# Retention, ELU MLP and maxout MLP on one core: weight conversion in four VectorE operations, tables moved ahead of the sums' loads, masks ahead of the updates

## The chip, the core and the metric

The kernel runs on one core of one Trainium2 chip. The metric is the device time of one execution in microseconds (us); the kernel before was timed in three runs, whose median counts.

## The reference, cut to what matters

```python
def _attn_ref(q, k, v):                          # B, H, S, D = 4, 8, 768, 64
    for t in range(S):
        state = gamma[None, :, None, None] * state + np.einsum('bhd,bhe->bhde', k[:, :, t], v[:, :, t])
        y[:, :, t] = scale * np.einsum('bhd,bhde->bhe', q[:, :, t], state)

def _moe_ref(x, w_in, w_out):                    # 512 -> 2048 -> 512
    h = x @ w_in
    g = np.where(h > 0.0, h, np.exp(np.minimum(h, 0.0)) - 1.0)
    return g @ w_out

def _moe2_ref(x, w1, w2, w3, w_out):             # 512 -> 768 (three times) -> 512
    return np.maximum(np.maximum(x @ w1, x @ w2), x @ w3) @ w_out

x = _attn_ref(q, k, v).transpose(0, 2, 1, 3).reshape(3072, 512)
out = _moe2_ref(_moe_ref(x, w_in, w_out), w1, w2, w3, w_out2)
```

q, k and v are float32; the weights come as 64-bit floats, so a weight is two 32-bit words in memory.

## The kernel before, in words

**Attention.** The 3072 tokens are 24 chunks of 128 (four sequences of six). A chunk is loaded by `load` (lines 90 and 98, on the SP queue). `keys_of` (L249, GpSimd) makes the decayed keys kd, `queries_of` (L260) the decayed queries qd. On TensorE a chunk takes `quarter_scores` (L271), `quarter_update` (L301, keys times values for the state), `quarter_values` (L341) and `past` (L328, queries times the earlier state). On VectorE `quarter_mask` (L283) multiplies the scores by the decay mask into the tile a, which `quarter_values` reads, and `carry` (L311 to L318) brings the state forward. `finish` (L356 on ScalarE, L359 on VectorE) writes the result as a high and a low part, xh and xl. Scores, updates, values and the MLP's hidden product hp take their PSUM from the same four-bank pool.

**MLP.** Matmuls run in fp32r. Every operand stands as a high and a low part, and a product is three passes: high by high, high by low, low by high. For a block b of 512 tokens and a group f of 128 hidden units, `h1` makes hp with 12 matmuls (L446), then e = exp on ScalarE (L453), a Relu (L454), the ELU on VectorE (L455), its high part gh on ScalarE (L456) and its low part gl on VectorE (L459). `o1` adds gh and gl times w_out into four accumulators with 12 matmuls (L478). At the end of a run of groups, `x2_out` adds the accumulators to earlier sums (L495) and, where a block is complete, stores them to the DRAM buffer x2d (L501, SP queue).

**Weights.** The weights of both MLPs are 56 half tiles of 128x512 double words. `load_half` (L369) brings one into the buffer raw (two buffers). The high part of w is the double's top bits as fp32, the low part the rest. Before, a half takes six VectorE operations and two ScalarE ones: `cv_bits` masks the high word (L382) and ScalarE rescales its exponent field as an integer (L385); `cv_rest` makes the remainder from both words (L392, L393); `cv_high` puts the sign in (L403), ScalarE casts to w's high part (L406); `cv_low` isolates the power of two (L412) and multiplies it in as w's low part (L413). The tiles t and m of these steps have two buffers each; `renew` (L852) uses the same tiles to bring stored partial sums back from x2d.

**Order.** The work is a list `seq` of (b, f). For its first 32 entries the weights come in while blocks 0 and 1 are computed (one half is converted at each entry, two at entries 2, 12 and 18), and the order on ScalarE and VectorE is that of the code; after entry 32 a scheduler sets it. TensorE's order is that of the code until the last h1/o1 product, and SP's always. In `third(i, part)` the six chunks 8 to 13 are laid by hand between the products of the first 32 entries. That function also sets when the tables are changed (`tables`: the decay mask at L231, and from chunk 12 on the swapped columns and rows at L234 and L235 with the reciprocal at L239 and a product at L243), and when the sums are renewed. `third(31, 0)`, the last of these calls, loads chunk 13, opens chunk 12, finishes chunk 11, changes the tables and carries chunk 12; after it come o1 of entry 31 and the x2_out that completes block 0. This place is called the seam below. In blocks 2 to 4 one chunk is done at each of twelve turns (`step`, `settle`).

Of the kernel before, what the change touches and what calls it, by code (L numbers as in the profile page):

```python
# [34 lines left out]
def kernel(ctx: ExitStack, tc: tile.TileContext, qkv0, qkv, wa, wb, dmask, qdec, cols, out):  # L35
# [187 lines left out]

    def twin():
        t = [ps_h.tile([P, 2, NPAIR, HC], F32, tag="h", name="xs") for _ in range(2)]
        return [y[:, 0] for y in t], [y[:, 1] for y in t]

    def tables(swapped):
        if not swapped:
# [12 lines left out]
        n = NPAIR // 2 if swapped else NPAIR  # L242
        nc.vector.tensor_tensor(out=late, in0=late, in1=by.unsqueeze(2).to_broadcast([P, n, HC]), op=ALU.mult)  # L243
# [132 lines left out]
    def cv_bits(n):  # L376
        if n // 2 >= len(keys):
            return
        t = dpool.tile([P, 512], I32, tag="t", name="t")
        m = dpool.tile([P, 512], F32, tag="m", name="m")  # L380
        tmp[n] = (t, m)
        nc.vector.tensor_scalar(  # L382
            out=t, in0=half[n][:, :, 1], scalar1=0x7FFFFE00, scalar2=None, op0=ALU.bitwise_and
        )
        nc.scalar.activation(t, t, ACTF.Relu, scale=8.0, bias=-896.0 * 2 ** 23)  # L385

    def cv_rest(n):
        if n // 2 >= len(keys):
            return
        m = tmp[n][1]  # L390
        lo, hi = half[n][:, :, 0].bitcast(U32), half[n][:, :, 1]
        nc.vector.tensor_scalar(out=m.bitcast(I32), in0=hi, scalar1=0x1FF, scalar2=None, op0=ALU.bitwise_and)  # L392
        nc.vector.scalar_tensor_tensor(  # L393
            out=m, in0=lo, scalar=2.0 ** -32, in1=m.bitcast(I32), op0=ALU.mult, op1=ALU.add
        )

    def cv_high(n):
        key, c = keys[n // 2], n % 2
        if c == 0:
            pool, tag = (ld, "r") if key[0] == "b" and key[1] == 0 else (wpool, "w")  # L400
            w_t[key] = pool.tile([P, 2, 2 * 512], F32R, tag=tag, name="w")
        t = tmp[n][0]
        nc.vector.scalar_tensor_tensor(  # L403
            out=t, in0=half[n][:, :, 1], scalar=-0x80000000, in1=t, op0=ALU.bitwise_and, op1=ALU.bitwise_or
        )
        nc.scalar.copy(w_t[key][:, 0, c * 512:(c + 1) * 512], f32(t))  # L406
        load_half(n + NSTAGE)

    def cv_low(n):
        key, c = keys[n // 2], n % 2  # L410
        t, m = tmp.pop(n)
# [51 lines left out]

    acc_t = {}

    def o1(b, f, f0, f1):
        g = g_t.pop((b, f))
        w = w_t["a", f]
        if f == f0:
            acc_t[b] = [ps_acc.tile([P, BLK], F32, tag="acc", name="acc") for _ in range(KDM)]  # L470
        order = [[(1, 0), (0, 0)], [(0, 1)]]
        if fresh(b, f):
            order = [[p] for p in FRESH]
        first, final = order[0][0], order[-1][-1]
        for passes in order:
            for m in range(KDM):
# [351 lines left out]
    def step(c):  # L828
# [2 lines left out]
        if b not in x_t:  # L831
            new_x(b)
        sc = twin()[0]
        xs, up = twin()
        quarter_scores(c + 1, sc)
        quarter_mask(c + 1)
        quarter_update(c + 1, up, True)
        quarter_values(c, xs)
        load(c + 2)

    def settle(c):
# [13 lines left out]
    def third(i, part):  # L855
        e, at_ = EARLY, (i - split, part)
        if at_ == (-10, 1):
            tables(False)
            load(e)
        if at_ == (-8, 1):  # L860
            load(e + 1)
            open_chunk(e)
            queries_of(e)
            carry(e)
        if at_ == (-6, 0):
            renew(1)
        if at_ == (-6, 1):
            quarter_values(e, twin()[0])
            load(e + 2)
        if at_ == (-5, 0):  # L870
            new_x(2)
        if at_ in {(-5, 0), (-4, 1), (-2, 0)}:
            c = {-5: e, -4: e + 1, -2: e + 2}[at_[0]]
            finish(c)
        if at_ in {(-5, 1), (-3, 0), (-2, 1)}:
            c = {-5: e + 1, -3: e + 2, -2: e + 3}[at_[0]]
            open_chunk(c)
            queries_of(c)
# [28 lines left out]
    for i, (b, f, f0, f1) in enumerate(seq):  # L907
# [143 lines left out]
```

## Time and profile before

| | |
|---|---|
| median of 3 runs | 1036.61 us (1035.41, 1036.61, 2502.99) |
| profiled execution | 1034.33 us |
| span on the core | 1032.6 us |
| mean granted TensorE clock | 0.991 |
| busy: PE / DVE / ACT | 993.1 / 646.3 / 361.6 us |

PE is TensorE's matmuls, PEld its weight loads, DVE VectorE, ACT ScalarE, POOL GpSimd and SP the engine that issues most DMAs. Times of rows are in us from the span's start. A row of a timeline gives start, busy time, engine, line, operation, output and inputs, shape, and in brackets how long the engine had been idle and what it waited for. A granted clock of 1.00 is 2.4 GHz, 0.50 is 1.2 GHz. The profiled execution's 1034.33 us are the span and 1.7 us around it.

### The profile page before, as it was taken

The page shows a single profiled execution, that of the slowest core. Times are in us where ns is not written, and L with a number is a line of the kernel's source. Part 1 is how long each engine was busy: PE and PEld are TensorE (multiplying, and loading weights), DVE is VectorE, ACT ScalarE, POOL GpSimd, SP SyncE. Part 2 cuts the span into 40 slices and gives each one's busy share as a digit, 9 for nine tenths or more (in the row PEclk, how much of TensorE's full clock was granted, in tenths as well). Part 3 has the DMA queues.
Part 4 walks back from the last instruction along what each step waited for, and adds up shares of the span by engine and source line. Part 5 has one row for each costly group of instructions (what it writes and reads, how often), then busy time and mean ns, then how long its engine had stood idle before and what let it go on. Part 6 is the DMA issues. An engine that isn't in the chain of part 4 may idle for free.

```text
span 1032.6 us, 17784 instructions
## 1 busy us (share of the span) xinstructions
PE 993.1 (96%) x7356; PEld 844.1 (82%) x7359; DVE 646.3 (63%) x1283; ACT 361.6 (35%) x713; POOL 46.3 (4%) x50
## 2 busy tenths in 40 slices
PE   7989999999699999999999999999999999999997
PEld 4767877777588888888888888888999999999996
DVE  3879899952533232333255899985876576756764
ACT  3456555431333333333344666432221021211211
POOL 0000000021111110111100000000000000000000
PEclk8999999999899999999999999999999999999999
DMA  9633333784111221112212244202002020010101
GB/s 245 173 95 111 102 104 111 229 221 129 56 45 45 58 87 42 42 42 83 83 42 72 92 143 155 71 1 82 1 2 82 1 72 11 21 62 1 42 2 41
DMA packets 62113, 79.94 MB, mean 77 GB/s; under 512 B 6224, under 2 KB 43344, under 8 KB 62032
## 3 DMA queue, kind: packets, MB, share of 16 engines
q1 hardware_dynamic: 56272, 68.31, 22.6%
q10 hardware_dynamic: 5760, 10.49, 2.7%
q8 instruction: 58, 0.95, 0.4%
q14 instruction: 23, 0.19, 0.1%
HBM read 64.10 MB, written 14.68 MB: 76 GB/s over the span
## 4 chain that ended last, share of the span: by engine, by line
PE 82%; DVE 11%; ACT 2%; DMA 2%; SPq 1%; issue 1%; POOL 0%; DVEq 0%; ACTq 0%; POOLq 0%
PE acc L478 22%; PE hp L446 22%; PE hp L656 19%; PE acc L705 8%; PE hp L546 5%; DVE xl L630 1%; DMA x<-in_qkv 1%; DVE t L663 1%; PE xs L341 1%; SPq L90 1%; PE xs L271 1%; DVE e L689 1%; PE xs L328 1%; DVE e L455 1%; DVE w L413 1%
## 5 line engine op out<-in xcount | busy, mean ns | idle before, releaser
L446 PE MATMUL hp<-xh,w 128*128 128x512 f32 x768 | 245.4, 392 | 5.6 <-DVE a L283 3.5
L656 PE MATMUL hp<-xh,w 128*128 128x256 f32 x1260 | 232.5, 283 | 2.0 <-DVE e L663 1.6
L478 PE MATMUL acc<-gh,w 128*128 128x512 f32 x768 | 198.1, 397 | 14.2 <-ACT gh L456 10.5
L656 PEld LDWEIGHTS hp<-xh,w 128*128 128x128 f32 x1260 | 198.1, 191 | 4.0 <-issue 1.4
L478 PEld LDWEIGHTS acc<-gh,w 128*128 128x128 f32 x768 | 142.6, 189 | 48.3 <-ACT gh L456 11.8
L656 PE MATMUL hp<-xl,w 128*128 128x256 f32 x630 | 178.9, 284 | 1.4 <-DVE xl L630 1.4
L446 PEld LDWEIGHTS hp<-xh,w 128*128 128x128 f32 x768 | 143.6, 188 | 37.8 <-DVE a L283 5.0
L455 DVE SCALAR_TENSOR_TENSOR e<-e,hp 128x512 f32<-128x512 f32 x96 | 65.8, 686 | 145.8 <-ACT e L454 144.9
L446 PE MATMUL hp<-xl,w 128*128 128x512 f32 x384 | 142.0, 390 | 0.0
L656 PEld LDWEIGHTS hp<-xl,w 128*128 128x128 f32 x630 | 120.0, 191 | 4.2 <-DVE xl L630 2.9
L453 ACT ACTIVATE e<-hp 128x512 f32<-128x512 f32 x96 | 57.1, 595 | 165.2 <-PE hp L446 162.7
L478 PE MATMUL acc<-gl,w 128*128 128x512 f32 x384 | 103.1, 390 | 0.0
L705 PE MATMUL acc<-w,gh 128*128 128x512 f32 x288 | 90.6, 391 | 0.0
L663 DVE TENSOR_TENSOR t<-hp,m 128x256 f32<-128x256 f32 (+1 forms) x90 | 45.9, 510 | 68.9 <-PE hp L656 68.3
L456 ACT CAST gh<-e 128x512 fp32r<-128x512 f32 x96 | 59.6, 621 | 79.9 <-DVE e L455 77.8
L459 DVE TENSOR_TENSOR gl<-e,gh 128x512 fp32r<-128x512 f32 x96 | 66.3, 691 | 32.4 <-ACT gh L456 30.1
L478 PEld LDWEIGHTS acc<-gl,w 128*128 128x128 f32 x384 | 72.4, 188 | 15.4
L446 PEld LDWEIGHTS hp<-xl,w 128*128 128x128 f32 x384 | 72.1, 188 | 14.8
L675 ACT COPY m<-hp 128x256 f32<-128x256 f32 x45 | 16.8, 374 | 189.6 <-PE hp L656 117.9
L705 PEld LDWEIGHTS acc<-w,gh 128*128 128x128 f32 x288 | 53.9, 188 | 10.0
L454 ACT ACTIVATE e<-e 128x512 f32<-128x512 f32 x96 | 60.9, 634 | 2.6
L705 PE MATMUL acc<-w,gl 128*128 128x512 f32 x144 | 56.4, 392 | 1.0 <-DVE gl L695 1.0
(111 smaller groups left out, 1084.5 us busy)
## 6 DMA issues: line engine op xcount, KB each, us to landing
raw<-in_wa SPq DMA_DIRECT2D x32, 512.0 KB, 3.6
x<-in_qkv SPq DMA_DIRECT2D x24, 512.0 KB, 4.5
raw<-in_wb SPq DMA_DIRECT2D x24, 512.0 KB, 3.6
x<-in_qkv SPq DMA_DIRECT2D x96, 64.0 KB, 2.3
raw<-x2d SPq DMA_DIRECT2D x12, 512.0 KB, 3.8
out<-o ACTq DMA_DIRECT2D x24, 256.0 KB, 2.0
x<-in_qkv SPq DMA_DIRECT2D x32, 128.0 KB, 4.5
x2d<-o ACTq DMA_DIRECT2D x16, 256.0 KB, 2.0
```

The source lines that it names most:

```text
L446: nc.tensor.matmul(hp, w[:, pw, kk * P:(kk + 1) * P], x[px][:, kk, :], start=k == 0, stop=k == len(order) - 1,)
L453: nc.scalar.activation(e, hp, ACTF.Exp)
L454: nc.scalar.activation(e, e, ACTF.Relu, scale=-1.0, bias=1.0)
L455: nc.vector.scalar_tensor_tensor(out=e, in0=e, scalar=-1.0, in1=hp, op0=ALU.mult, op1=ALU.max)
L456: nc.scalar.copy(gh, e)
L459: nc.vector.tensor_tensor(out=gl, in0=e, in1=f32(gh), op=ALU.subtract)
L478: nc.tensor.matmul(acc_t[b][m], w[:, p[0], 512 + m * P:512 + (m + 1) * P], g[p[1]], start=f == f0 and p == first, stop=f == f1 - 1 and p = ...
L546: nc.tensor.matmul(hp, w[:, pw, c0:c0 + P], x[px][:, kk, :], start=k == 0, stop=k == 3 * KDM - 1)
L656: nc.tensor.matmul(o, ws[i][:, pw, kk * P:(kk + 1) * P], xs[i][px][:, kk, :], start=first and k == 0, stop=last and k == 5,)
L663: nc.vector.tensor_tensor(out=out, in0=a, in1=c, op=ALU.add)
L675: nc.scalar.copy(u, pa[:, :HB])
L705: nc.tensor.matmul(acc_t[NB + b][m], g[px][:, m * P:(m + 1) * P], w[:, pw, 512:1024], start=f == 0 and i == 0, stop=f == KF2 - 1 and i == 2,)
```

## The change

Four parts.

1. A conversion takes four VectorE operations. ScalarE scales the high word, read as an fp32, by 2^-112 straight out of raw (L393 of the changed kernel). VectorE shifts the result left by three and clears the sign bit (L400), puts the sign in (L403), puts the top three bits of the low word in by a shift to the right (L406); ScalarE casts to w's high part (L417), and VectorE subtracts that from t to get w's low part (L422). The next `load_half` is now called after L406.
2. In the first 32 entries the table transfers come ahead of the sums' loads, loads of chunks ahead of tables, and kd and qd are made earlier. The reciprocal and the product of the swapped tables stay where they were.
3. In a turn of blocks 2 to 4 TensorE does scores, values, past, update, and the mask's wait on the old values comes ahead of the update. The two small copies that guard the banks become one that reads both.
4. The last o1 before the seam's sums is cut: m 0 and 1 ahead of `third(31, 0)`, m 2 and 3 behind it.

```diff
+    def tables(swapped, arrived=False):
+        if arrived:
+            pass
+        elif not swapped:
...
+        if swapped and not arrived:
+            return
...
         past(c, 0)
+
+    def fence(c, both):
         for s in range(c % NCH == 0, 2):
-            nc.scalar.copy(guard[:, s:s + 1], banks[s][:, 0, 0:1])
+            n = 2 if c + 1 < NCHUNK else 1
+            nc.scalar.copy(guard[:, 2 * s:2 * s + n], both[s][:, 0:n, 0, 0])
...
     def cv_bits(n):
-        nc.vector.tensor_scalar(
-            out=t, in0=half[n][:, :, 1], scalar1=0x7FFFFE00, scalar2=None, op0=ALU.bitwise_and
-        )
-        nc.scalar.activation(t, t, ACTF.Relu, scale=8.0, bias=-896.0 * 2 ** 23)
+        t = tmp[n] = dpool.tile([P, 512], I32, tag="t", name="t")
+        nc.scalar.activation(f32(t), f32(half[n][:, :, 1]), ACTF.Copy, scale=2.0 ** -112)
 
     def cv_rest(n):
-        nc.vector.tensor_scalar(out=m.bitcast(I32), in0=hi, scalar1=0x1FF, scalar2=None, op0=ALU.bitwise_and)
+        nc.vector.tensor_scalar(
+            out=t, in0=t, scalar1=3, scalar2=0x7FFFFFFF, op0=ALU.logical_shift_left, op1=ALU.bitwise_and
+        )
         nc.vector.scalar_tensor_tensor(
-            out=m, in0=lo, scalar=2.0 ** -32, in1=m.bitcast(I32), op0=ALU.mult, op1=ALU.add
+            out=t, in0=hi, scalar=-0x80000000, in1=t, op0=ALU.bitwise_and, op1=ALU.bitwise_or
         )
+        nc.vector.scalar_tensor_tensor(
+            out=t.bitcast(U32), in0=lo.bitcast(U32), scalar=29, in1=t.bitcast(U32),
+            op0=ALU.logical_shift_right, op1=ALU.bitwise_or,
+        )
+        load_half(n + NSTAGE)
 
     def cv_high(n):
-        nc.vector.scalar_tensor_tensor(
-            out=t, in0=half[n][:, :, 1], scalar=-0x80000000, in1=t, op0=ALU.bitwise_and, op1=ALU.bitwise_or
-        )
-        nc.scalar.copy(w_t[key][:, 0, c * 512:(c + 1) * 512], f32(t))
-        load_half(n + NSTAGE)
+        nc.scalar.copy(w_t[key][:, 0, c * 512:(c + 1) * 512], f32(tmp[n]))
 
     def cv_low(n):
-        nc.vector.tensor_scalar(out=t, in0=t, scalar1=-0x800000, scalar2=None, op0=ALU.bitwise_and)
-        nc.vector.scalar_tensor_tensor(
-            out=w_t[key][:, 1, c * 512:(c + 1) * 512], in0=m, scalar=2.0 ** -20, in1=f32(t),
-            op0=ALU.mult, op1=ALU.mult,
-        )
+        w = w_t[key][:, :, c * 512:(c + 1) * 512]
+        nc.vector.tensor_tensor(out=w[:, 1], in0=f32(tmp.pop(n)), in1=f32(w[:, 0]), op=ALU.subtract)
...
     def step(c):
...
         quarter_scores(c + 1, sc)
+        quarter_values(c, xs)
         quarter_mask(c + 1)
-        quarter_update(c + 1, up, True)
-        quarter_values(c, xs)
+        quarter_update(c + 1, up, False)
+        fence(c, both)
...
         if at_ == (-2, 1):
+            tables(True)
             renew(0)
         if at_ == (-1, 0):
-            quarter_values(e + 3, twin()[0])
+            lone_values(e + 3)
             load(e + 5)
             open_chunk(e + 4)
             finish(e + 3)
-            tables(True)
+            tables(True, True)
...
         if i == split - 1:
+            o1(b, f, f0, f1, (0, 1))
             third(i, 0)
-            o1(b, f, f0, f1)
+            o1(b, f, f0, f1, (2, 3))
             x2_out(b, f0, f1, False)
```

On SP's queue at the seam, the rows of before from the last of the sums' loads (L852) to the first store of a sum (L501); L90 and L98 are the load of chunk 13, L234 and L235 the swapped tables:

```order
L852 DMA m<-x2d 128x512
L90 DMA x<-in_qkv 64x2x128 x8
L98 DMA x<-in_qkv 128x4x256
L234 DMA qdec_sb<-in_qdec 64x2x128
L235 DMA cols_sb<-in_cols 64x2x1
L234 DMA qdec_sb<-in_qdec 64x2x128
L235 DMA cols_sb<-in_cols 64x2x1
L501 DMA x2d<-t 128x512
```

The same place after, from the end of the load of chunk 12; L236 and L237 are the tables, L858 the sums' loads, L507 the store:

```order
L98 DMA x<-in_qkv 128x4x256
L236 DMA qdec_sb<-in_qdec 64x2x128
L237 DMA cols_sb<-in_cols 64x2x1
L236 DMA qdec_sb<-in_qdec 64x2x128
L237 DMA cols_sb<-in_cols 64x2x1
L858 DMA t<-x2d 128x512
L858 DMA m<-x2d 128x512
L858 DMA t<-x2d 128x512
L858 DMA m<-x2d 128x512
L90 DMA x<-in_qkv 64x2x128 x8
L98 DMA x<-in_qkv 128x4x256
L507 DMA x2d<-t 128x512
```

The four table transfers stood between the load of chunk 13 and the store; they now stand ahead of the sums' loads, and the load of chunk 13 is the last thing ahead of the store.

On TensorE at a turn, before (L271 scores, L301 update, L341 values, L328 the part of the earlier state, L446 the next hidden product):

```order
L271 MATMUL xs<-x 64x64 x16
L301 MATMUL xs<-x,kd 64x64 x16
L341 MATMUL xs<-a,x 64x64 x16
L328 MATMUL xs<-qd,dmask_sb 64x64 x4
L446 MATMUL hp<-xh,w 128x512
```

And after, under the changed kernel's line numbers (L275, L345, L332, L305, L452 in that order):

```order
L275 MATMUL xs<-x 64x64 x16
L345 MATMUL xs<-a,x 64x64 x16
L332 MATMUL xs<-qd,dmask_sb 64x64 x4
L305 MATMUL xs<-x,kd 64x64 x16
L452 MATMUL hp<-xh,w 128x512
```

The update moved from the second place to the last one ahead of the hidden product.

On VectorE in the first 32 entries, one entry before, behind an earlier add (L412 and L413 end one half, the rows behind them convert the next; L455 and L459 are the ELU and gl):

```order
L412 TENSOR_SCALAR t<-t 128x512
L413 SCALAR_TENSOR_TENSOR w<-m,t 128x512
L392 TENSOR_SCALAR m<-raw 128x512
L393 SCALAR_TENSOR_TENSOR m<-raw,m 128x512
L455 SCALAR_TENSOR_TENSOR e<-e,hp 128x512
L403 SCALAR_TENSOR_TENSOR t<-raw,t 128x512
L459 TENSOR_TENSOR gl<-e,gh 128x512
L382 TENSOR_SCALAR t<-raw 128x512
```

And one entry after (L422 ends a half; L461 and L465 are the ELU and gl):

```order
L422 TENSOR_TENSOR w<-t,w 128x512
L400 TENSOR_SCALAR t<-t 128x512
L403 SCALAR_TENSOR_TENSOR t<-raw,t 128x512
L406 SCALAR_TENSOR_TENSOR t<-raw,t 128x512
L461 SCALAR_TENSOR_TENSOR e<-e,hp 128x512
L465 TENSOR_TENSOR gl<-e,gh 128x512
```

Nothing stands between the ELU and gl any more, and nothing of a conversion behind gl.

## Rows read from the trace of the kernel before

**Rows 1.** The page's part 1: engine, busy us, share of the span, instructions.

```profile
PE 993.1 (96%) x7356; PEld 844.1 (82%) x7359; DVE 646.3 (63%) x1283; ACT 361.6 (35%) x713; POOL 46.3 (4%) x50
```

**Rows 2.** Windows: us, PE, PEld, DVE, ACT, POOL busy, clock, DMA share, GB/s.

```profile
600.00:700.00 100.00, 100.00 (x442) 82.80 (x442) 90.70 (x202) 47.90 (x91) 0.00 (x0) 1.00 0.26 85
```

**Rows 3.** Waits of PE: engine, line, waited for: us in total, times, longest.

```profile
PE hp L446 <- DVE a L283: 3.5, 11, 0.3
PE hp L446 <- ACT w L406: 2.1, 2, 1.6
```

**Rows 4.** Groups of instructions on DVE: shapes, count | busy, mean ns | idle before.

```profile
L459 DVE TENSOR_TENSOR gl<-e,gh 128x512 fp32r<-128x512 f32 x96 | 66.3, 691 | 32.4 <-ACT gh L456 30.1
...
L403 DVE SCALAR_TENSOR_TENSOR t<-raw,t 128x512 int32<-128x512 int32 x56 | 38.8, 693 | 0.0
L382 DVE TENSOR_SCALAR t<-raw 128x512 int32<-128x512 int32 x56 | 24.7, 441 | 2.9 <-DMA raw<-in_wb 2.4 <-DMA x2d<-t 0.4
```

**Rows 5.** The same of ACT.

```profile
L385 ACT ACTIVATE t<-t 128x512 int32<-128x512 int32 x56 | 35.4, 631 | 40.1 <-DVE t L382 39.8
```

**Rows 6.** Timelines of DVE and PE in the first 32 entries, where PE waits.

```profile
83.33 0.96 PE L478 MATMUL acc<-gh,w 128*128 128x512 f32 x3 [0.48 <-ACT gh L456]
...
138.42 0.42 DVE L382 TENSOR_SCALAR t<-raw 128x512 int32<-128x512 int32 x1
138.75 2.48 DVE L495 TENSOR_TENSOR part<-acc,part 128x512 f32<-128x512 f32 x4
...
139.59 2.44 PE L478 MATMUL acc<-gh,w 128*128 128x512 f32 x8 [1.57 <-ACT t L385]
...
174.06 1.20 PE L478 MATMUL acc<-gh,w 128*128 128x512 f32 x4 [1.20 <-ACT gh L456]
...
196.53 1.24 PE L478 MATMUL acc<-gh,w 128*128 128x512 f32 x4 [0.31 <-ACT t L385]
```

**Rows 7.** Timeline of SP's queue at the seam.

```profile
242.50 0.59 SPq L98 DMA_DIRECT2D x<-in_qkv  x1
...
246.19 5.72 SPq L90 DMA_DIRECT2D x<-in_qkv  x8
...
252.59 0.55 SPq L234 DMA_DIRECT2D qdec_sb<-in_qdec  x1
...
255.09 0.60 SPq L235 DMA_DIRECT2D cols_sb<-in_cols  x1
259.75 0.33 SPq L501 DMA_DIRECT2D x2d<-t  x1
```

**Rows 8.** Timelines of DVE and PE at the seam.

```profile
257.77 0.18 DVE L239 RECIPROCAL cols_sb<-cols_sb 128x4 f32<-128x4 f32 x1 [7.43 <-DMA cols_sb<-in_cols]
...
259.04 0.68 DVE L495 TENSOR_TENSOR t<-acc,t 128x512 f32<-128x512 f32 x1
...
261.89 0.43 DVE L382 TENSOR_SCALAR t<-raw 128x512 int32<-128x512 int32 x1 [0.38 <-DMA x2d<-t]
...
266.35 3.78 PE L478 MATMUL acc<-gh,w 128*128 128x512 f32 x8 [8.84 <-ACT gh L456]
...
273.79 1.98 PE L478 MATMUL acc<-gh,w 128*128 128x512 f32 x8
```

**Rows 9.** SP's issues of the sums (ns min/median/max) and a store's landing (KB, us).

```profile
L852 SPq DMA_DIRECT2D m<-x2d x4: 430/432/683, 209.5 to 244.6; - x4
...
x2d<-part SPq DMA_DIRECT2D x8, 256.0 KB, 4.6
```

**Rows 10.** Windows behind the seam, columns as in rows 2.

```profile
264.00:266.00 2.00, 0.00 (x0) 0.00 (x0) 2.00 (x5) 1.45 (x4) 0.00 (x0) 0.50 0.00 0
...
271.00:272.00 1.00, 1.00 (x6) 0.78 (x6) 0.00 (x0) 0.00 (x0) 0.00 (x0) 1.00 0.00 0
```

**Rows 11.** Timelines of DVE and PE at one turn.

```profile
303.13 0.76 DVE L283 TENSOR_TENSOR a<-xs,dmask_sb 128x256 f32<-128x256 f32 x2 [0.95 <-PE xs L341]
...
303.61 0.50 PE L446 MATMUL hp<-xh,w 128*128 128x512 f32 x1 [0.31 <-DVE a L283]
```

More of the change, by code (lines that the diff above doesn't have):

```diff
@@ L225, in twin @@
         t = [ps_h.tile([P, 2, NPAIR, HC], F32, tag="h", name="xs") for _ in range(2)]
-        return [y[:, 0] for y in t], [y[:, 1] for y in t]
-    def tables(swapped):
-        if not swapped:
+        return [y[:, 0] for y in t], [y[:, 1] for y in t], t
+    def tables(swapped, arrived=False):
+        if arrived:
+            pass
+        elif not swapped:
             for s in range(2):
@@ L345, in quarter_values, with lone_values @@
         past(c, 0)
+    def fence(c, both):
         for s in range(c % NCH == 0, 2):
-            nc.scalar.copy(guard[:, s:s + 1], banks[s][:, 0, 0:1])
+            n = 2 if c + 1 < NCHUNK else 1
+            nc.scalar.copy(guard[:, 2 * s:2 * s + n], both[s][:, 0:n, 0, 0])
+    def lone_values(c):
+        xs, _, both = twin()
+        quarter_values(c, xs)
+        for s in range(c % NCH == 0, 2):
+            nc.scalar.copy(guard[:, 2 * s:2 * s + 1], both[s][:, 0, 0, 0:1])
     def finish(c):
@@ L378, in cv_bits @@
             return
-        t = dpool.tile([P, 512], I32, tag="t", name="t")
-        m = dpool.tile([P, 512], F32, tag="m", name="m")
-        tmp[n] = (t, m)
-        nc.vector.tensor_scalar(
-            out=t, in0=half[n][:, :, 1], scalar1=0x7FFFFE00, scalar2=None, op0=ALU.bitwise_and
-        )
-        nc.scalar.activation(t, t, ACTF.Relu, scale=8.0, bias=-896.0 * 2 ** 23)
+        t = tmp[n] = dpool.tile([P, 512], I32, tag="t", name="t")
+        nc.scalar.activation(f32(t), f32(half[n][:, :, 1]), ACTF.Copy, scale=2.0 ** -112)
     def cv_rest(n):
@@ L389, in cv_rest @@
             return
-        m = tmp[n][1]
-        lo, hi = half[n][:, :, 0].bitcast(U32), half[n][:, :, 1]
-        nc.vector.tensor_scalar(out=m.bitcast(I32), in0=hi, scalar1=0x1FF, scalar2=None, op0=ALU.bitwise_and)
+        t = tmp[n]
+        lo, hi = half[n][:, :, 0], half[n][:, :, 1]
+        nc.vector.tensor_scalar(
+            out=t, in0=t, scalar1=3, scalar2=0x7FFFFFFF, op0=ALU.logical_shift_left, op1=ALU.bitwise_and
+        )
         nc.vector.scalar_tensor_tensor(
-            out=m, in0=lo, scalar=2.0 ** -32, in1=m.bitcast(I32), op0=ALU.mult, op1=ALU.add
+            out=t, in0=hi, scalar=-0x80000000, in1=t, op0=ALU.bitwise_and, op1=ALU.bitwise_or
         )
+        nc.vector.scalar_tensor_tensor(
[3 more added lines that the diff above has]
+        load_half(n + NSTAGE)
     def cv_high(n):
@@ L464, with o1 @@
     acc_t = {}
-    def o1(b, f, f0, f1):
-        g = g_t.pop((b, f))
+    def o1(b, f, f0, f1, ms=range(KDM)):
+        g = g_t[b, f]
         w = w_t["a", f]
-        if f == f0:
+        if f == f0 and 0 in ms:
             acc_t[b] = [ps_acc.tile([P, BLK], F32, tag="acc", name="acc") for _ in range(KDM)]
@@ L475, in o1 @@
         for passes in order:
-            for m in range(KDM):
+            for m in ms:
                 for p in passes:
@@ L821, in open_chunk @@
     def open_chunk(c):
-        sc, up = twin()
-        keys_of(c)
+        sc, up, _ = twin()
         quarter_scores(c, sc)
@@ L833, in step @@
         sc = twin()[0]
-        xs, up = twin()
+        xs, up, both = twin()
         quarter_scores(c + 1, sc)
+        quarter_values(c, xs)
         quarter_mask(c + 1)
-        quarter_update(c + 1, up, True)
-        quarter_values(c, xs)
+        quarter_update(c + 1, up, False)
+        fence(c, both)
         load(c + 2)
@@ L857, in third @@
         if at_ == (-10, 1):
+            load(e)
             tables(False)
-            load(e)
+        if at_ == (-9, 1):
+            keys_of(e)
+            queries_of(e)
         if at_ == (-8, 1):
@@ L862, in third @@
             open_chunk(e)
-            queries_of(e)
             carry(e)
+            keys_of(e + 1)
         if at_ == (-6, 0):
@@ L867, in third @@
         if at_ == (-6, 1):
-            quarter_values(e, twin()[0])
+            lone_values(e)
             load(e + 2)
@@ L874, in third @@
             finish(c)
+            queries_of(c + 1)
         if at_ in {(-5, 1), (-3, 0), (-2, 1)}:
@@ L877, in third @@
             open_chunk(c)
-            queries_of(c)
             carry(c)
+            keys_of(c + 1)
         if at_ in {(-4, 0), (-3, 1)}:
             c = {-4: e + 1, -3: e + 2}[at_[0]]
-            quarter_values(c, twin()[0])
+            lone_values(c)
             load(c + 2)
         if at_ == (-2, 1):
+            tables(True)
             renew(0)
         if at_ == (-1, 0):
-            quarter_values(e + 3, twin()[0])
+            lone_values(e + 3)
             load(e + 5)
```

2 lines of the change are left out of this document (removed).

## The prediction

> **What bounds the kernel now.** I read the page's busy times first. TensorE's matmuls are busy for 993.1 us [rows 1] of a span of 1032.6, so 39.5 us are idle; the other engines are far from full. In a stretch of the middle they have no idle time at all, with VectorE at 90.7% beside them [rows 2]: the 442 matmuls of 100 us stand 0.226 us apart, and an entry of the list, an h1 and an o1 with 24 matmuls, takes 5.43 us. There, less work on VectorE is worth nothing. The change can win only where TensorE waits, or where its clock is low.
>
> So next the waits of TensorE, and the timeline at each. Waits for weights stand at the start [rows 3]: 2.1 us in two pieces, of 1.6 and 0.5. In the first 32 entries four short waits are for gh, or are listed under t of L385 [rows 6]: 0.48, 1.57, 1.20 and 0.31 us, 3.56 together. The second and fourth of these end when the accumulators have been added to the sums; that they carry the name of L385 comes from the way releasers are inferred. At the seam is the largest, 8.84 us up to 266.35 [rows 8]. Behind it the clock is at 0.50 [rows 10], the lower of the two levels: the first eight matmuls take 3.78 us, the same eight later 1.98 [rows 8], and with the few behind them the low clock costs some 2.0 us; it is at 1.00 again from 271 on [rows 10]. Eleven times the hidden product waits for the mask, 3.5 us in all [rows 3], 0.31 each [rows 11].
>
> The chain at the seam, by SP's queue [rows 7] and VectorE [rows 8]: the load of chunk 13 is issued from 246.19 on, the four table transfers from 252.59 to 255.69; the tables' landing ends a wait of 7.43 us of the reciprocal at 257.77; it stands ahead of the sums' adds in VectorE's queue, which so begin only at 259.04; their first store is issued at 259.75; the next conversion needs the tile t and begins at 261.89, when the store has landed 2.14 us after its issue; from there to TensorE's restart at 266.35 another 4.46 us go by through conversion, exp, ELU and gh.
>
> **Part 1, the conversions.** Before, three operations like L382 (0.441 us) and three like L403 (0.693) [rows 4]: 3.40 us for a half. After, one of the first kind and three of the second or of the kind of L459 (0.691) [rows 4]: 2.52. That is 0.88 us less, 49 us of VectorE for 56 halves. Most of it is hidden. An entry on VectorE took two operations of the ELU and a conversion, 1.38 + 3.40 = 4.78; L403 stood in the gap in which ScalarE makes gh. Now the gap is empty; with 0.63 for it, from ScalarE's nearest row [rows 5], the entry takes 1.38 + 0.63 + 2.52 = 4.53. Both are below TensorE's 5.43. What counts are the entries with two conversions and those with adds, where VectorE falls behind. There I take half of 0.88, since L403 of the first one filled a gap: 0.44 off each of the waits at 83.33, 139.59 and 174.06. At the second and fourth wait the add also stood behind L382 (0.33 from its start to that of the add) [rows 6]; this operation is gone from there: 0.33 and 0.31 more. Together -2.0 us. The ends are 0 (VectorE was behind for another reason) and -3.56 (all four waits go).
>
> At the start the first half has no cover. After ScalarE's step its cast waited for one operation of 0.69; now for 0.44 + 0.69 + 0.69 = 1.82, so +1.1. The second wait, 0.5, should vanish, as the next halves are ready earlier: +0.6 net. Ends: 0 and +1.1.
>
> Shifts as such are in no row of before. By the rows all 32-bit operations of one form cost the same whatever they compute, 0.441 and 0.69; from below an operation that is not faster than these, from above twice the price, 0.88 and 1.38. I take the rows' price, which is the nearest in form; twice the price is the third rival. The Trainium skill, page "VectorE: DVE Perf Modes", section "The perf-mode tier table", puts fp32 tensor_scalar in SBUF at the second tier and tensor_tensor at the first; the trace agrees, 0.441 against 0.691. By that rule a shift of this form stays at 0.44, and if it has no such tier it takes 0.69, 0.25 more for a half, which is hidden in an entry of 4.53 and adds 0.25 at the start alone.
>
> ScalarE now reads raw with a step of two words. No row of ScalarE shows that; VectorE's L403 reads the same words at 0.693, no slower than L459 reads adjacent ones [rows 4]. I take 0.63 as for L385 [rows 5]; below, nothing less; above, twice, 1.26. ScalarE is busy 35% [rows 1], so even that counts only where nothing covers it, once at the start and twice at the seam: +1.9. The Trainium skill, page "SBUF — State Buffer", section "Door 1: The DMA port swizzle", says that accesses within one 16-byte line go at full bandwidth from two hits a line on, and that each crossing to a new line pays. A step of two words leaves just two hits, so by its first half the sum stays at -9.1, and if the crossings do pay, it is -7.2; no run so far shows which.
>
> **Part 2, the seam.** With the tables ahead of the sums' loads, the reciprocal finds them landed and the adds are ready some 7 us earlier. But the order of SP's queue now has the whole load of chunk 13 ahead of the first store, and that load takes 6.4 us to issue (246.19 to 252.59) [rows 7]. Ahead of it SP now issues the tables (3.1 us, 252.59 to 255.69) and the sums' loads (four of some 0.43 to 0.5 [rows 9], 1.9 us), from 243.1, the end of the load of chunk 12 (242.50 + 0.59 [rows 7]), which stands right ahead of them. So 243.1 + 3.1 + 1.9 = 248.1 and + 6.4 = 254.4 or a little later: the store is issued 5.35 us sooner than at 259.75. That is the step on which the term rests: SP, not the adds, holds the store back. From there the chain is a little longer: ScalarE's two conversion steps both stand ahead of the next exp and each waits for a store, so I count 4.9 us to the restart for 4.46 before, +0.45. The store's landing will be slower, as the data of chunk 13 are still moving when it is issued: 2.14 before, 4.6 for such a store elsewhere [rows 9]; I take +0.7, as the issue spreads the load over 6 us and most of it is in. Net -4.2; the ends are -3.0 (landing of 4.1) and -7.0 (SP doesn't hold the store). About 4.6 us of stall are left, and after a shorter idle time at the seam's length I have no row with a high clock: the 2.0 us of low clock stay, and their going is the end below.
>
> The cut o1 gives the tensor engine six matmuls ahead of the attention rather than behind it, the same work, and lies in front of the same stall; kd and qd earlier likewise. Both 0, covered by that stall, which SP's chain ends whatever TensorE did before; without the stall they would be worth less than the other waits in reach, of 0.3 to 1.6 us [rows 6].
>
> **Part 3, the turns.** The mask at 303.13 waits 0.95 us for the values, which read the tile that it overwrites, and the hidden product waits 0.31 for it [rows 11]. With the values ahead of the update, the mask has the update's 16 matmul pairs beside it, longer than 0.31, and the wait goes: -3.5 for eleven. What is late next is nothing I can see: the hidden product's other inputs are long there. Ends: -3.5 and 0.
>
> **Behind entry 32** the scheduler orders conversions of the last 24 halves anew, beside a full TensorE: 0. As no row shows what a new order costs there, I bound it by one wait of the length of those of rows 6, plus or minus 1.5.
>
> **The sum** against the profiled execution of 1034.33: -2.0 + 0.6 - 4.2 - 3.5 = -9.1, so 1025.2. The two usable runs stand 1.1 and 2.3 us above that execution; I add 1.7 and give 1027.0.
>
> **The rivals.**
> First, SP doesn't hold the store, because the load goes out faster or the stores land at once. For it speaks that the reciprocal's wait of 7.43 us, ahead of the adds, goes wholly; against, the order on SP. Then the seam gives 7.0, and a stall of 2 us may leave the clock up, 2.0 more: 1034.3 - 2.0 + 0.6 - 7.0 - 2.0 - 3.5 + 1.7 = 1022.
> Second, only the seam gains: VectorE's waits are those of the adds themselves, and in the turns the hidden product finds another wait, such as PSUM held by the update that now comes last. 1034.3 + 0.6 - 4.2 + 1.7 = 1032.4. For it speaks that such waits are short and chained, against it that row by row a named releaser moves.
> Third, slower than before: VectorE's shifts at twice the price. L400 takes 0.88 and L406 1.38, 1.13 more for a half; an entry takes 4.53 + 1.13 = 5.66, above TensorE's 5.43. It decides from 0.9 us more on, which is the slack. Then each of some 30 entries loses 0.2 (6 us), and the 20 adds of the sums, 0.60 apart (2.48 for four [rows 6]), lose their cover: 12 us. 1034.3 + 18 + 0.6 - 4.2 - 3.5 + 1.7 = 1047; the three second conversions could add some 10. Against it: no 32-bit row of VectorE shows such a price.
>
> **How the numbers follow.** The forecast has a chance of 0.54, the first rival 0.20, the second 0.20, the third 0.06. The lower end takes all favourable ends: 1034.3 - 3.6 - 7.0 - 2.0 - 3.5 - 1.5 + 1.1 = 1018. The upper one all bad ones but the third rival: 1034.3 + 1.1 - 3.0 + 1.5 + 2.3 = 1036. About what a measurement of this kernel can tell from no change is 2%, 20.7 us; below 1015.9 only ends that go further than mine would lead, 0.05; above 1057.3 the worst of the third rival, 0.03; the rest is within.
>
> **What would show it.** Right: the reciprocal without a wait; the first store directly behind the load of chunk 13 on SP's queue at about 254; TensorE's wait for gh there at 4 to 5 us and the clock still down; no wait of L452 for a; VectorE some 49 us less busy with the middle of the run unchanged; the first wait for w about 1 us longer. Wrong: the store far from that load's end, L400 or L406 well above 0.44 and 0.69, L393 above 0.63, or new waits of TensorE in the last third of the run.

## The result and the profile after

The changed kernel takes 1042.72 us (median of 4 runs, 1042.13 to 1043.80); the kernel before, measured beside it, 1036.80. The ratio is 1.0063, with a 95% interval of 1.0043 to 1.0082: slower by 0.6%, where 1027 was forecast. One of the four runs of the kernel before took 2502.99 us and is left out of the ratio. The profiled execution took 1043.8 us, its span 1042.0, 9.4 us more than before; the mean clock fell from 0.991 to 0.985.

The page's part 1 of the changed kernel, the answer to [rows 1]:

```profile
PE 1000.5 (96%) x7356; PEld 848.8 (81%) x7359; DVE 612.1 (59%) x1171; ACT 357.8 (34%) x713; POOL 46.9 (4%) x50
```

VectorE is 34 us less busy, where 49 was forecast; why is said below, at part 1. TensorE is 7.4 us busier with the same 7356 instructions: it ran longer at the low clock (mean 0.985 for 0.991). Idle it is 41.5 us for 39.5 before.

Its waits, the answer to [rows 3]:

```profile
PE acc L484 <- ACT gh L462: 18.6, 7, 7.6
...
PE hp L452 <- ACT w L417: 2.7, 1, 2.7
```

The wait for the mask is gone. The waits for gh were 10.5 us in three; they are 18.6 in seven, and the largest is only 7.6: new ones have come in. Where they stand is seen best from a ledger. ScalarE's cast gh exists once for each entry, 96 times in both kernels, and its start in the one trace less its start in the other tells how far behind the changed kernel is. A ledger sets one execution against one other: three kernels of the experiments that leave the start as it was stand at -1.3, -0.4 and +0.9 us at the first gh, so a single place is good to about 1 us.

| place | before | after | behind by | change of it |
|---|---|---|---|---|
| first gh | 40.75 | 43.73 | +2.98 | +2.98 the start |
| 32nd gh, ahead of the seam | 241.97 | 241.88 | -0.09 | -3.07 the conversions |
| 36th gh, past the seam | 284.04 | 281.73 | -2.31 | -2.2 the seam |
| 43rd and 46th | 325.66, 345.00 | 322.93, 349.27 | -2.73, +4.27 | +7.0 new stall |
| 63rd and 66th | 449.67, 469.05 | 452.30, 476.87 | +2.63, +7.82 | +5.2 new stall |
| 77th | 538.00 | 544.63 | +6.63 | turns in between, -3.3 |
| last product of the run | | | +9.44 | +2.8 behind entry 77 |

**The new stalls.** Timelines of the first one, GpSimd and VectorE before, then GpSimd, VectorE and TensorE after (the last row is the second stall):

```profile
331.93 0.61 POOL L313 TENSOR_TENSOR dmask_sb<-state,cols_sb 128x256 f32<-128x256 f32 x1 [17.30 <-DMA x<-in_qkv]
332.50 1.29 POOL L260 TENSOR_TENSOR qd<-x,qdec_sb 128x512 f32<-128x512 f32 x1
...
332.91 0.69 DVE L455 SCALAR_TENSOR_TENSOR e<-e,hp 128x512 f32<-128x512 f32 x1
...
333.85 0.41 DVE L316 TENSOR_TENSOR dmask_sb<-xs,dmask_sb 128x256 f32<-128x256 f32 x1
...
338.76 1.05 POOL L249 TENSOR_TENSOR kd<-x,cols_sb 128x512 f32<-128x512 f32 x1 [4.96 <-DMA x<-in_qkv]
```

```profile
335.26 1.04 POOL L253 TENSOR_TENSOR kd<-x,cols_sb 128x512 f32<-128x512 f32 x1 [23.77 <-DMA x<-in_qkv]
336.26 0.61 POOL L317 TENSOR_TENSOR dmask_sb<-state,cols_sb 128x256 f32<-128x256 f32 x1
...
336.90 0.42 DVE L320 TENSOR_TENSOR dmask_sb<-xs,dmask_sb 128x256 f32<-128x256 f32 x1 [6.88 <-POOL dmask_sb L317]
337.24 0.68 DVE L461 SCALAR_TENSOR_TENSOR e<-e,hp 128x512 f32<-128x512 f32 x1
...
338.62 3.78 PE L484 MATMUL acc<-gh,w 128*128 128x512 f32 x8 [4.23 <-ACT gh L462]
...
467.48 3.67 PE L484 MATMUL acc<-gh,w 128*128 128x512 f32 x8 [3.71 <-ACT gh L462]
```

Before, GpSimd did the carry's product (L313), then qd, then kd of the chunk after, which waits for that chunk's load. After, kd stands first. The load is issued at the turn itself, so GpSimd waits for it until 335.26, the carry's product is late by that, VectorE waits 6.88 us for it, and behind VectorE's L320 stands the ELU that TensorE needs. No line of the diff moves this: the scheduler did.

Two queues have changed here, not one. Before, VectorE's ELU (L455, 332.91) stood ahead of the carry's add (L316, 333.85), so a late product could not have held it back; now L320 stands ahead of the ELU, at both stalled turns and at no other turn of the changed kernel. On GpSimd kd stands first at three turns (335.26, 415.31 and 464.11); at the middle one no carry stands behind it, and nothing stalls.

Behind the stall the clock is low:

```profile
336.00:338.00 2.00, 0.00 (x0) 0.00 (x0) 1.10 (x3) 0.05 (x1) 2.00 (x3) 0.98 0.00 0
338.00:340.00 2.00, 1.38 (x3) 1.16 (x4) 1.18 (x3) 1.70 (x3) 0.09 (x1) 0.50 0.00 0
```

That is 1.2 GHz from 338 on (columns as in rows 2), and the eight matmuls take 3.78 us, as behind the seam.

**The start.** TensorE and ScalarE at the first w, and the clock behind:

```profile
33.79 0.67 ACT L393 ACTIVATE t<-raw 128x512 f32<-128x512 f32 x1
36.41 0.62 ACT L417 CAST w<-t 128x512 fp32r<-128x512 f32 x1 [1.95 <-DVE t L406]
37.08 1.69 PE L452 MATMUL hp<-xh,w 128*128 128x512 f32 x4 [2.72 <-ACT w L417]
...
38.00:40.00 2.00, 2.00 (x6) 1.52 (x6) 1.93 (x4) 1.51 (x7) 0.00 (x0) 0.50 0.89 276
```

The same wait and the clock behind it before:

```profile
35.68 1.19 PE L446 MATMUL hp<-xh,w 128*128 128x512 f32 x4 [1.57 <-ACT w L406]
...
36.00:38.00 2.00, 2.00 (x10) 1.64 (x9) 1.93 (x5) 2.00 (x9) 0.00 (x0) 1.00 0.77 243
```

The wait is 1.15 us longer than before. Behind it the clock falls, which it had not done behind the 1.6 us of before, and the first twelve matmuls take 4.5 us (37.08 to 41.62) for 3.0. The fall isn't certain: seven traces of this document have this wait at 2.7 us, and in six of them the clock falls and the twelve matmuls take 4.2 to 4.5 us. In the seventh, the change without the turns' edit (below), it stays up and they take 2.9:

```profile
36.90 1.20 PE L457 MATMUL hp<-xh,w 128*128 128x512 f32 x4 [2.71 <-ACT w L422]
...
38.00:40.00 2.00, 2.00 (x13) 1.41 (x13) 1.97 (x4) 1.39 (x7) 0.00 (x0) 1.00 0.91 258
```

**The seam**, the answer to [rows 7, 8]:

```profile
249.96 0.17 DVE L243 RECIPROCAL cols_sb<-cols_sb 128x4 f32<-128x4 f32 x1
...
251.22 0.68 DVE L501 TENSOR_TENSOR t<-acc,t 128x512 f32<-128x512 f32 x1
...
253.39 0.59 SPq L98 DMA_DIRECT2D x<-in_qkv  x1
254.08 0.45 SPq L507 DMA_DIRECT2D x2d<-t  x1
...
258.52 0.66 ACT L393 ACTIVATE t<-raw 128x512 f32<-128x512 f32 x1 [9.00 <-DMA x2d<-t]
...
263.46 3.78 PE L484 MATMUL acc<-gh,w 128*128 128x512 f32 x8 [7.59 <-ACT gh L462]
```

The reciprocal waits for nothing and the first add is done at 251.9; the store stands right behind the load of chunk 13, at 254.08, and lands only 4.4 us later, at 258.5.

**The end of the first MLP.** ScalarE's waits there, and two new ones of TensorE:

```profile
ACT t L393 <- DMA raw<-in_wb: 16.3, 15, 2.1
...
629.40 2.11 PE L484 MATMUL acc<-gh,w 128*128 128x512 f32 x8 [1.25 <-ACT gh L462]
...
641.21 2.11 PE L484 MATMUL acc<-gh,w 128*128 128x512 f32 x8 [0.62 <-ACT gh L462]
```

ScalarE now reads raw first, and so waits for its transfers; before, it was VectorE, for 2.4 us [rows 4].

### The profile page after: what moved, and what is told of

Its sections match the earlier page's. It is cut to its first block, busy times and chain, and to the rows that moved or that the text cites. A ratio compares the mean times of both kernels' runs of the same rounds, so it can differ in the third digit from the quotient of the medians.

```text
span 1042.0 us, 17721 instructions
## 1 busy us (share of the span) xinstructions
PE 1000.5 (96%) x7356; PEld 848.8 (81%) x7359; DVE 612.1 (59%) x1171; ACT 357.8 (34%) x713; POOL 46.9 (4%) x50
## 4 chain that ended last, share of the span: by engine, by line
PE 76%; DVE 10%; DMA 6%; SPq 3%; ACT 2%; issue 1%; POOL 0%; ACTq 0%; POOLq 0%; DVEq 0%
PE acc L484 21%; PE hp L662 19%; PE hp L452 18%; PE acc L711 8%; PE hp L552 5%; DMA raw<-in_wb 3%; SPq L90 2%; DMA x<-in_qkv 2%; DVE xl L636 1%; DVE t L403 1%; DVE t L669 1%; DVE t L406 1%; PE xs L275 1%; DVE e L695 1%; PE xs L332 1%
## 5 line engine op out<-in xcount | busy, mean ns | idle before, releaser
L452 PE MATMUL hp<-xh,w 128*128 128x512 f32 x768 | 245.7, 394 | 2.8 <-ACT w L417 2.7
L484 PE MATMUL acc<-gh,w 128*128 128x512 f32 x768 | 202.4, 402 | 20.9 <-ACT gh L462 18.6
L452 PEld LDWEIGHTS hp<-xh,w 128*128 128x128 f32 x768 | 144.9, 189 | 34.3 <-ACT w L417 3.2
L461 DVE SCALAR_TENSOR_TENSOR e<-e,hp 128x512 f32<-128x512 f32 x96 | 65.7, 685 | 146.0 <-ACT e L460 145.1
L452 PE MATMUL hp<-xl,w 128*128 128x512 f32 x384 | 143.0, 393 | 0.0
L459 ACT ACTIVATE e<-hp 128x512 f32<-128x512 f32 x96 | 57.1, 595 | 166.6 <-PE hp L452 165.2
L465 DVE TENSOR_TENSOR gl<-e,gh 128x512 fp32r<-128x512 f32 x96 | 66.3, 691 | 48.9 <-ACT gh L462 48.2
L452 PEld LDWEIGHTS hp<-xl,w 128*128 128x128 f32 x384 | 73.0, 190 | 15.1
```

What stands on the lines that cost most here:

```text
L452: nc.tensor.matmul(hp, w[:, pw, kk * P:(kk + 1) * P], x[px][:, kk, :], start=k == 0, stop=k == len(order) - 1,)
L459: nc.scalar.activation(e, hp, ACTF.Exp)
L461: nc.vector.scalar_tensor_tensor(out=e, in0=e, scalar=-1.0, in1=hp, op0=ALU.mult, op1=ALU.max)
L465: nc.vector.tensor_tensor(out=gl, in0=e, in1=f32(gh), op=ALU.subtract)
L484: nc.tensor.matmul(acc_t[b][m], w[:, p[0], 512 + m * P:512 + (m + 1) * P], g[p[1]], start=f == f0 and p == first, stop=f == f1 - 1 and p = ...
```

## The experiments

Every ratio is against runs of the kernel before on the same chip. First the three parts, each alone, and the one order that the diff doesn't show.

**GpSimd's order by hand.** On the changed kernel; its code has qd, the carry's product, kd in this order.

```diff
         if i == split:
             start.__exit__(None, None, None)
+            hand = tc.manual_schedule(engines={mybir.EngineType.Pool})
+            hand.__enter__()
         if i == last:
+            hand.__exit__(None, None, None)
             products.__exit__(None, None, None)
```

> The changed kernel with GpSimd's order written by hand from entry 32 on: qd, the carry's product, then kd of the next chunk. Theory: the two stalls of TensorE at turns (4.2 and 3.7 us, each with a low clock behind it) come from kd standing ahead of the carry's product on GpSimd; they go, no wait of VectorE for the product above 1 us is left there, and the time falls by 7.0 + 5.2 us to about 1031. Rival: the stalls come from TensorE's new order at the turn itself (the update last); then they stay wherever GpSimd's order is, and the time stays at 1042 to 1043.

Measured 1030.07 us, ratio 0.9944 (0.9927 to 0.9960). GpSimd at the same turn, in the same view:

```profile
330.54 1.30 POOL L264 TENSOR_TENSOR qd<-x,qdec_sb 128x512 f32<-128x512 f32 x1 [17.77 <-PE xs L332]
331.78 0.62 POOL L317 TENSOR_TENSOR dmask_sb<-state,cols_sb 128x256 f32<-128x256 f32 x1
336.77 1.05 POOL L253 TENSOR_TENSOR kd<-x,cols_sb 128x512 f32<-128x512 f32 x1 [4.37 <-DMA x<-in_qkv]
```

kd waits as before, with nothing behind it, and both stalls are gone: VectorE waits 0.6 us in all for the carry's product, for 13.8 in the changed kernel. TensorE's order at the turn is unchanged, so the rival falls. VectorE's order came back with it: its ELU is again ahead of the carry's add.

**The conversions alone**, the four functions put into the kernel before.

> The kernel before with the four conversion functions alone changed. Theory: the conversions lose 3.0 us at the start (a wait of 2.7 us and a low clock behind it), win 3.1 up to entry 32 and lose 2.8 where ScalarE waits for raw behind entry 70: 1036.8 + 2.7 = about 1039.5, and no wait of VectorE for GpSimd at a turn. Rival: the conversions, by moving ScalarE's work, also make the stalls at the turns: then about 1050. My forecast's own term (-2.0 + 0.6) would give 1035.4.

Measured 1034.97 us, ratio 1.0000 (0.9990 to 1.0009). By the ledger of its trace the places are as expected: +2.8 at the first gh, -3.5 up to the 32nd, +3.0 behind entry 80. The ledger ends at +1.6, and the timed runs show no difference at all: the places were right, the 2.7 us of the sum were not. (The profiled executions are not typical here: that of the kernel before, 1034.33 us, is faster than all but one of its 19 runs beside this experiment, and this one's is 1.0 us above its median.) The wait of VectorE for GpSimd is 0.6 us in all, so the conversions don't make the stalls.

**The turns alone**, `step`, `fence` and the guard copies that go with it put into the kernel before.

> The kernel before with the turns alone changed (values and mask ahead of the update, the fence). Theory: the wait of the hidden product for the mask goes, 0.42 us at each of eleven turns, but the scheduler moves kd ahead of the carry's product on GpSimd at some turns, and each such stall costs 5 to 7 us with its low clock: two of them give 1036.8 - 4.2 + 12 = about 1045. Rival: the stalls need the new conversions; then 1036.8 - 4.2 = about 1032.5.

Measured 1042.46 us, ratio 1.0065 (1.0045 to 1.0085). VectorE's waits for the carry's product, one of them by itself, and TensorE's two stalls:

```profile
DVE dmask_sb L316 <- POOL dmask_sb L313: 19.3, 4, 6.8
...
341.64 3.78 PE L487 MATMUL acc<-gh,w 128*128 128x512 f32 x8 [4.14 <-ACT gh L465]
...
445.58 0.42 DVE L316 TENSOR_TENSOR dmask_sb<-xs,dmask_sb 128x256 f32<-128x256 f32 x1 [5.90 <-POOL dmask_sb L313]
...
496.00 1.20 PE L487 MATMUL acc<-gl,w 128*128 128x512 f32 x4 [2.77 <-DVE gl L468]
```

This edit alone makes the kernel as slow as the whole change does, through the same rows. It also shows what VectorE's order is worth. kd stands ahead of the carry's product at three turns. At the first the add is ahead of the ELU, and TensorE stalls for 4.14 us; at the other two the ELU is ahead, and TensorE waits 2.77 us for gl at one and not at all at the other (445.58), although VectorE has waited 5.90 us.

**The turns, with GpSimd's order by hand**, the same five lines as above.

> The kernel before with the turns' edit and GpSimd's order by hand. Theory: the edit is worth what was forecast once GpSimd's order is kept, eleven or twelve times 0.4 us: 4 to 5 us below the kernel before. Rival: half of that is given back by GpSimd's fixed order (qd ahead of the carry's product); then 1 to 2 us below it.

Measured 1031.80 us, ratio 0.9963 (0.9950 to 0.9975), 3.8 us faster than before: the edit's gain is what the eleven waits were worth, with no sign of the rival's loss. GpSimd's order by hand on the kernel before alone was not run; there VectorE waits only 0.6 us in all for the carry's product. Between the two kernels lie 10.6 us by the ratios, and one order written by hand on an engine that is busy 4% of the time.

**The change without the turns' edit**, the old `step` in the changed kernel.

> The changed kernel with the turns of the kernel before (scores, mask, update, values), all else as changed and GpSimd's order left to the scheduler. Theory: without the turns' edit the scheduler keeps kd behind the carry's product, no stall is left at the turns, the waits of 0.31 us for the mask are back, and the time is that of the kernel before plus the seam's gain and the conversions' zero: 1 to 2 us below it. Rival: the other parts stall the turns too; then 1040 or more.

Measured 1035.99 us, ratio 0.9998 (0.9987 to 1.0009). No stall at the turns: VectorE waits 0.6 us for the carry's product. The gain of 1 to 2 us was a miss: here conversions and seam together give nothing. With GpSimd's order by hand the same two parts are worth 2.0 us by the ratios (0.9944 against 0.9963), but those intervals overlap.

**The seam alone**, `tables`, `third` and the cut o1 in the kernel before.

> The kernel before with the seam alone changed (tables, kd, qd and loads moved in the first 32 entries, the last o1 cut). Theory: the store is issued right behind the load of chunk 13, its landing takes about 4.3 us instead of 2.1, and TensorE restarts 2.2 to 3 us sooner: 1036.8 - 2.6 = about 1034. Rival: the gain at the seam is made by the new conversions, which both start ahead of the exp; then within 1 us of 1036.8.

Measured 1034.18 us, ratio 0.9984 (0.9974 to 0.9994): 1.7 us, without the new conversions. That speaks against the rival, but the interval is 0.6 to 2.7 us, so a gain below its 1 us is not excluded; the gain is smaller than expected. The store was issued at 257.56 and landed 4.9 us later.

Now the losses that were left, each on top of the kernel with GpSimd's order by hand (ratio 0.9944).

**The first conversion early.**

```diff
+        if c + 1 == CB:
+            cv_bits(0)
+            cv_rest(0)
         end(c)
...
-    cv_bits(0)
-    cv_rest(0)
     rest(CB - 1)
```

> The kernel with GpSimd's order by hand, and the first half's scale and three VectorE operations ahead of the last of the first four chunks' ends, where both engines wait. Theory: the wait for the first w falls from 2.7 us to at most 0.6, the clock stays up behind it (1.6 us), and the time falls by 3 to 4 us against the kernel with the order alone, to about 1026.5. Rival: the clock's fall there and the start's 3 us are the spread of the first transfers from run to run; then within 1 us of 1030.

Measured 1027.55 us, ratio 0.9912 (0.9896 to 0.9927), 3.3 us better by the ratios (the two intervals just touch). The first hidden product waits for nothing and takes its full clock:

```profile
33.66 0.62 ACT L417 CAST w<-t 128x512 fp32r<-128x512 f32 x1
...
34.33 1.20 PE L452 MATMUL hp<-xh,w 128*128 128x512 f32 x4
```

**The load of chunk 13 behind the stores.**

```diff
             lone_values(e + 3)
-            load(e + 5)
...
-            keys_of(e + 5)
...
             x2_out(b, f0, f1, False)
+            load(EARLY + 5)
+            keys_of(EARLY + 5)
```

> The kernel with GpSimd's order by hand, and the load of chunk 13 behind the stores of the sums in SP's queue. Theory: SP holds the stores back, and their landing is slow beside that load; now the store is issued at about 252, lands 2.1 us later, and TensorE restarts some 5 us sooner, at about 260: 1030 - 5 = 1025, and 2 us less again if the clock stays up. Rival: the load of chunk 13, now later, holds up the first turn, and the gain is given back there: 1029 to 1031.

Measured 1025.83 us, ratio 0.9894 (0.9876 to 0.9912), 5.2 us better. SP, ScalarE, TensorE and the clock:

```profile
252.31 0.32 SPq L507 DMA_DIRECT2D x2d<-t  x1
...
254.79 0.66 ACT L393 ACTIVATE t<-raw 128x512 f32<-128x512 f32 x1 [4.88 <-DMA x2d<-t]
...
259.73 2.75 PE L484 MATMUL acc<-gh,w 128*128 128x512 f32 x8 [3.46 <-ACT gh L462]
...
260.00:262.00 2.00, 2.00 (x8) 1.58 (x8) 1.32 (x3) 0.82 (x2) 0.00 (x0) 0.74 0.55 116
```

In the kernel with the order alone the store was issued at 255.62, landed 4.9 us later, and TensorE restarted at 265.48:

```profile
255.62 0.45 SPq L507 DMA_DIRECT2D x2d<-t  x1
...
265.48 3.78 PE L484 MATMUL acc<-gh,w 128*128 128x512 f32 x8 [9.00 <-ACT gh L462]
```

Now it is issued 3.3 us sooner, which is SP's share, it lands after 2.5 us, and TensorE restarts at 259.73, 5.75 us sooner. The clock still falls, to 0.74 in the window behind, after an idle time of 3.5 us. The first turn gives nothing back.

**The last 24 halves by the old conversion.** The four old functions are kept beside the new ones, and `make` calls them.

> The kernel with GpSimd's order by hand, and the old six-operation conversion for the last 24 halves (those of the second MLP). Theory: with the old conversion VectorE is the first to read raw, ScalarE has no wait for a transfer, and the 3.9 us lost between entry 70 and the end of the first MLP come back: 1030 - 3.9 = about 1026. Rival: they are lost to something else of the changed order; then 1029 to 1031.

Measured 1029.39 us, ratio 0.9924 (0.9904 to 0.9945).

**The last 24 halves by the new conversion, the scale on VectorE.**

```diff
-        nc.scalar.activation(f32(t), f32(half[n][:, :, 1]), ACTF.Copy, scale=2.0 ** -112)
+        if n < 2 * KFF:
+            nc.scalar.activation(f32(t), f32(half[n][:, :, 1]), ACTF.Copy, scale=2.0 ** -112)
+        else:
+            nc.vector.tensor_scalar(
+                out=f32(t), in0=f32(half[n][:, :, 1]), scalar1=2.0 ** -112, scalar2=None, op0=ALU.mult
+            )
```

> The same last 24 halves by the new conversion, but with the scale by 2^-112 on VectorE (a tensor_scalar of some 0.44 us) in the place of ScalarE. Theory: what costs is that ScalarE, whose queue holds exp and gh, is the first reader of raw and waits for its transfer; on VectorE the same wait costs little, and the time is that of the old conversion there, about 1026. Rival: what costs is the chain's length or raw coming free later, which this leaves as it is: 1029 to 1031.

Measured 1028.85 us, ratio 0.9930 (0.9912 to 0.9948). By the timed runs the two are 2.1 and 1.5 us better than the order alone, but the intervals overlap with its own, so a time alone doesn't settle it. The traces do: from the 80th gh on the kernel with ScalarE's scale loses 3.9 us (from -5.40 to -1.51 against before), that with the old conversion 0.1 (-8.37 to -8.30), that with VectorE's scale none (-6.23 to -6.29). The other traces agree: behind the 80th gh the six with the new conversion and ScalarE's scale there lose 2.1 to 3.9 us, the four with the old conversion or VectorE's scale in its place at most 0.4. VectorE's waits for raw in the last:

```profile
L396 DVE TENSOR_SCALAR t<-raw 128x512 f32<-128x512 f32 x24 | 10.3, 434 | 11.4 <-DMA raw<-in_wb 6.0 <-DMA x2d<-t 5.4
```

The wait is still there, 6.0 us (16.3 on ScalarE in the changed kernel), on an engine whose queue doesn't lead to gh at once. In the profiles, then, the loss goes with the wait's place, ScalarE's queue; its size lies between 1.5 us and 3.9. The profiled execution with the old conversion, 1026.0 us, was 3.3 us faster than the other three of that kernel, so what it loses behind entry 80 counts here, and not its total.

**All of it together**, with the old conversion for the last 24 halves, and with VectorE's scale there.

> The changed kernel with GpSimd's order by hand, the first half's conversion early, the load of chunk 13 behind the stores, and the old conversion for the last 24 halves. If the gains add, 3.3 + 5.2 + 2 us below the kernel with the order alone: about 1019.5 to 1021. If two of them come from the same idle time, 1023 to 1026.

> The same with the new conversion for the last 24 halves, its scale on VectorE. Theory as for the old conversion there: within 1.5 us of it, about 1020 to 1022.

Measured 1017.79 us, ratio 0.9832 (0.9806 to 0.9857), and 1019.82, ratio 0.9846 (0.9814 to 0.9877); the 2 us between them are within the intervals. The gains add: 0.9944 less 0.0032, 0.0050 and 0.0020 would be 0.9842. The first is 1.7% faster than the kernel before. TensorE in it, by the page and by its longest wait for gh at the seam:

```profile
PE 993.4 (97%) x7356; PEld 845.0 (83%) x7359; DVE 624.9 (61%) x1219; ACT 358.8 (35%) x713; POOL 47.5 (5%) x50
...
257.64 3.48 PE L526 MATMUL acc<-gh,w 128*128 128x512 f32 x8 [3.05 <-ACT gh L504]
```

## Why the prediction was wrong

**Part 3, "What is late next is nothing I can see".** This is the step that failed, together with "Behind entry 32 ... 0", bounded by 1.5 us. The term itself was right: -3.5 forecast, 3.8 us measured once GpSimd's order is kept, about 0.42 a turn in the trace. But I followed the wait on the engines that it names, TensorE and VectorE, and did not look at how the scheduler would set GpSimd's queue once the update had moved. It put kd, which waits for a load issued at the same turn, ahead of the carry's product, and VectorE's add of the carry ahead of the ELU. Two stalls of TensorE of about 4 us, with a low clock behind each, cost 12 us in the ledger; the turn's edit alone went from 3.8 us faster to 6.9 slower. My rival for the slower side, shifts at twice the price, was the wrong one. Why the scheduler's choice flips stays open; that the edit of `step` with its `fence` alone flips it was shown.

**Part 1, the conversions.** The shifts cost what the rows of like form said: L400 0.42 us, L403 0.70, L406 0.71, and ScalarE's strided read 0.67 for 0.63, so none of the doubled prices was paid. These are their groups:

```profile
L406 DVE SCALAR_TENSOR_TENSOR t<-raw,t 128x512 uint32<-128x512 uint32 x56 | 39.5, 707 | 1.4
...
L400 DVE TENSOR_SCALAR t<-t 128x512 int32<-128x512 int32 x56 | 23.6, 422 | 16.5 <-ACT t L393 16.3
...
L393 ACT ACTIVATE t<-raw 128x512 f32<-128x512 f32 x56 | 37.4, 670 | 26.3 <-DMA raw<-in_wb 16.3 <-DMA x2d<-t 9.6 <-DVE w L422 0.3
```

The Trainium skill (page "SBUF — State Buffer", section "Door 1: The DMA port swizzle") says that accesses within one 16-byte line go at full bandwidth from two hits a line on. The trace nearly agrees: 0.670 us for L393, which reads at a step of two words, against 0.631 for L385, another operation on adjacent words.

VectorE's 49 us were mis-sized. The durations of the conversions' rows add up to 49 us less, but rows that follow each other overlap (in [rows 6] L382 starts at 138.42, lasts 0.42 and the next row starts at 138.75), and two rows fewer save only 0.61 us of busy time for a half and not 0.88: 34 us in all.

The four waits that the term names, 3.56 us, are 2.03 now, so -1.5 for -2.0; the fourth is gone. With half of 0.61 in place of half of 0.88 the term would have come out at -1.6. The three that are left:

```profile
85.48 1.19 PE L484 MATMUL acc<-gh,w 128*128 128x512 f32 x4 [0.52 <-ACT gh L462]
...
140.99 2.44 PE L484 MATMUL acc<-gh,w 128*128 128x512 f32 x8 [0.81 <-DVE part L501]
...
174.97 1.19 PE L484 MATMUL acc<-gh,w 128*128 128x512 f32 x4 [0.70 <-ACT gh L462]
```

The ledger's -3.1 for that stretch (-3.5 with the conversions alone) also has the second wait for w, which vanishes as forecast. The start was mis-sized, +1.1 for +3.0: the first wait is 1.15 us longer, as forecast, but the fall of the clock behind it, 1.6 us, was not in the sum, and the rest is within the spread. The late weights I had bounded by the scheduler's order and not by the engine that waits for raw; they lose 2.8 us (3.5 behind entry 80).

**Part 2, the seam.** Right in its mechanism: the reciprocal doesn't wait, SP holds the store back until 254.08 (254.4 forecast), and from the landing to the restart 4.9 us go by (4.9 forecast). The landing was the mis-sized term, 4.4 us for 2.8, and behind the shorter stall the clock stays low a little longer, 0.7 us: -2.2 in place of -4.2. TensorE's wait there is 7.59 us and not some 4.6, because it also begins sooner (255.87 for 257.52); its end is what counts. The -2.2 is one trace: in the seven traces with this order of SP's queue the same stretch of the ledger gives -0.4 to -3.6. Putting the load behind the stores gives 5.2 us back, which shows that it was that load.

So the sum by the ledger is +3.0 - 3.1 - 2.2 - 3.3 + 12.2 + 2.8 = +9.4 us; without the 12.2 the change would have been 2.8 us faster in its profile, and was 5.8 us faster in time with GpSimd's order kept. The parts alone add up to about that, by the ratios: 3.8 us for the turns with the order by hand, 1.7 for the seam, nothing for the conversions.

## What to carry to other kernels

Where a scheduler sets the order, compare every engine's queue before and after an edit, the idle engines too: one instruction that waits for a transfer, put ahead of one that is needed, stalls the kernel from an engine that is busy 4% of the time. Look then at what stands behind the late result in the next engine's queue: with the ELU behind it TensorE stalled for about 4 us, with the ELU ahead of it for 2.77 or not at all. The first reader of a loaded buffer should be on an engine whose queue doesn't feed the bound engine soon. Stores that release a buffer belong ahead of loads that nobody needs yet.

## What was not expected of the hardware

The clock's fall has a price of its own that can exceed the wait's: the first wait for w grew from 1.57 to 2.72 us, and the twelve matmuls behind it from 3.0 to 4.5, at a granted clock of 0.50. The length of the wait alone doesn't settle it: behind 2.7 us the clock fell in six traces and stayed at 1.00 in one, with 2.9 us for the twelve matmuls. A store of 256 KB that is issued right behind a chunk's load landed after 4.4 to 4.9 us, and ahead of the load after 2.5.
